# Loading the first eight chunks of a retention kernel in three transfers each, with masks by pairs and a new order of conversions

## The chip, the cores and the metric

The kernel runs on one core of a Trainium2 chip. The metric is the device time of one execution in microseconds (us), the median of several runs. Names of engines: PE is TensorE (matmuls), PEld its weight loads, DVE is VectorE, ACT is ScalarE, POOL is GpSimd, and SP is the engine whose queue issues nearly all loads here.

## What is computed

A retention layer (a linear attention with decay) feeds two dense layers one after the other. Sizes: 4 batches, 8 heads, 768 tokens, head width 64; so 3072 tokens of width 512.

```python
for t in range(S):
    state = gamma[None, :, None, None] * state + np.einsum('bhd,bhe->bhde', k[:, :, t], v[:, :, t])
    y[:, :, t] = scale * np.einsum('bhd,bhde->bhe', q[:, :, t], state)
...
h = x @ w_in                                    # 512 -> 2048
g = np.where(h > 0.0, h, alpha * (np.exp(np.minimum(h, 0.0)) - 1.0))
x = g @ w_out                                   # 2048 -> 512
...
h = np.maximum(np.maximum(x @ w1, x @ w2), x @ w3)   # 512 -> 768, three times
return (h @ w_out).astype(np.float32)
```

The weights arrive as 64-bit floats, and the kernel makes 32-bit ones of them on the chip, as a high and a low part.

## The kernel before

**Chunks.** The retention goes over chunks of 128 tokens with all 8 heads (four pairs); six chunks make a batch, four make a block of 512 tokens for the dense layers. A chunk's tile `x` (1 MB) holds four slots for each pair of heads: queries, keys, keys by token, values by token. For chunk c the kernel forms scores (keys times queries), masks them with the decay table `dmask` (tile `a`), multiplies by the values into `xo` ("mix"; `values` in the later form), adds the state's part by `qd`, the scaled queries ("past"), and carries the state on with an update `up` from `kd`, the scaled keys. `xo` is then split into a high part `xh` (ACT) and a low part `xl` (DVE), which the first dense layer reads.

**Forms.** Chunks 0 to 3 (block 0) use the functions `wide_...`, later ones `open_chunk`, `values`, `finish`, `ready`. The first eight chunks come from an input of their own, `qkv0`, in which the queries lie twice, padded with zeros.

**Weights.** `load_half(n)` loads the n-th half of a weight tile (512 KB) into `raw`, with two buffers. `cv_bits(n)` (ACT) and `cv_rest(n)` (three DVE instructions) turn it into a 32-bit float in `t`, and `cv_rest` then issues the load of half n+2. `cv_high(n)` (ACT) and `cv_low(n)` (DVE) write the two parts into `w`. Halves 0 and 1 serve step f = 0 of the first dense layer, halves 2 and 3 step f = 1, half 4 and on the next ones.

**Dense layer one.** `h1(b, f)` is 12 matmuls of block b with the first half of the weights into `hp`, then on ACT two steps and on DVE one that make `e`, and the split of `e` into `gh` and `gl`. `o1(b, f, ...)` is 12 matmuls with the second half into the accumulators `acc`. On a tile's first use (`fresh`) the passes go in the order in which the parts come ready, the low part of the weights last. `x2_out` copies the four accumulators out at a group's end, and only then can the next group of `o1` begin.

**Order.** The order of the work on every engine up to the last groups is that in which the code is written; every engine runs its own instructions in that order and waits where one isn't ready. The SP queue is in that order too, and each of its transfers waits for the one eight before it to land. PE runs the same list of matmuls throughout: junk products before the first data, chunks 0 to 3, then `h1(0, 0)`, `o1(0, 0)`, `h1(0, 1)`, `o1(0, 1)` with chunks 4 to 7 between them, then `h1(1, 0)`, `h1(1, 1)`, `o1(1, 0)`, `h1(1, 2)` and so on. Past about 200 us nothing of the change is left in the order.

Of the kernel before, what the change touches and what calls it, by code (L numbers as in the profile page):

```python
# [34 lines left out]
def kernel(ctx: ExitStack, tc: tile.TileContext, qkv0, qkv, wa, wb, dmask, qdec, cols, out):  # L35
# [32 lines left out]
    def load(c, part=None):  # L68


        if c >= NCHUNK:
# [4 lines left out]
        if part != 1:
            if c in raw_t:
                return
            if early:
                x = wpool.tile([P, NPAIR, 4, P], F32, tag="w", name="x")  # L80
            else:
                x = ld.tile([P, NPAIR, 4, P], F32, tag="r", name="x")
            raw_t[c] = x
            if early:
                for h, at_, o, n in ((rows(0), 0, 0, 1), (rows(0), 1, 2, 1), (rows(1), 0, 1, 2)):
                    nc.sync.dma_start(
                        out=x[h, :, at_:at_ + n, :].rearrange("d p s t -> d p (s t)"),
                        in_=src[c, :, h, o * P:(o + n) * P].rearrange("p d t -> d p t"),
                    )
            else:  # L90
                for g in range(2):
                    for s in range(2):
                        for p in range(1 if c < 2 * NCH else 2):
                            ps = slice(None) if c < 2 * NCH else slice(p, None, 2)
                            cc = slice((2 * s + (g ^ p)) * P, (2 * s + (g ^ p) + 1) * P)
                            nc.sync.dma_start(
                                out=x[rows(g), ps, s, :], in_=src[c, ps, rows(g), cc].rearrange("p d t -> d p t")
                            )
# [894 lines left out]
```

## Time and profile before

| | before |
|---|---|
| median of 3 runs | 1016.08 us (1013.62 to 1018.23) |
| the profiled execution, its own time | 1016.3 us |
| its span in the trace | 1014.5 us |
| PE busy | 985.0 us, 97% of the span |
| DVE, ACT, POOL busy | 606.2, 348.9, 67.1 us |
| mean granted TensorE clock | 0.996 |

The busy time says who has the most work, not what a change is worth. For that one reads the stretch that the change touches, here the first 80 us or so, and there the idle time of PE and what ended it.

### The profile page before, as it was taken

Reading aid. Unit: us, or ns where it says so; the run is one execution under the profiler, and the core shown is the slowest. Engines: PE = TensorE matmul, PEld = TensorE weight load, DVE = VectorE, ACT = ScalarE, POOL = GpSimd, SP = SyncE. Lnnn points to the kernel's source line nnn. Section 1 sums busy time; section 2 is a strip of 40 time slices with the busy share of each in tenths; the row PEclk is TensorE's granted clock in tenths of the full one; section 3 lists DMA queues with packets and bytes.
Section 4 is the critical chain, followed back from the end, with each engine's and each line's share of the span. In section 5 each row is a group of like instructions: output and inputs, shape, how many; then the busy total and the mean of one; then the engine's idle time right before and its main releaser. Section 6 shows DMA issues by size and latency. Waiting matters only on the chain.

```text
span 1014.5 us, 18210 instructions
## 1 busy us (share of the span) xinstructions
PE 985.0 (97%) x7616; PEld 841.5 (83%) x7616; DVE 606.2 (60%) x1187; ACT 348.9 (34%) x669; POOL 67.1 (7%) x68
## 2 busy tenths in 40 slices
PE   7889999999999999999999999999999999999997
PEld 4667887777888888888888887888999999899996
DVE  2867888744333323333335887997875676757764
ACT  1445555533333333333334665432221121211211
POOL 2410001021111110111100000000000000000000
PEclk9999999999999999999999999999999999999999
DMA  9913364454211211121102444302001020110101
GB/s 236 237 59 103 104 188 161 136 182 127 88 43 43 84 43 42 43 84 43 43 1 87 143 145 146 105 1 83 2 26 58 2 78 6 42 43 1 43 1 42
DMA packets 59010, 79.70 MB, mean 79 GB/s; under 512 B 5168, under 2 KB 40240, under 8 KB 58928
## 3 DMA queue, kind: packets, MB, share of 16 engines
q1 hardware_dynamic: 53168, 68.05, 22.7%
q10 hardware_dynamic: 5760, 10.49, 2.8%
q8 instruction: 60, 0.98, 0.4%
q14 instruction: 22, 0.18, 0.1%
HBM read 63.84 MB, written 14.68 MB: 77 GB/s over the span
## 4 chain that ended last, share of the span: by engine, by line
PE 74%; DVE 13%; DMA 5%; ACT 4%; issue 2%; SPq 1%; POOL 1%; ACTq 0%; DVEq 0%; POOLq 0%
PE hp L612 19%; PE hp L396 19%; PE acc L430 19%; PE acc L661 8%; PE hp L501 5%; DMA raw<-in_wb 3%; DVE t L347 2%; DVE xl L586 1%; ACT gh L408 1%; DVE t L350 1%; DVE e L407 1%; DVE t L619 1%; PE xs L217 1%; PE xs L160 1%; DVE gl L411 1%
## 5 line engine op out<-in xcount | busy, mean ns | idle before, releaser
L396 PE MATMUL hp<-xh,w 128*128 128x512 f32 x768 | 243.7, 390 | 3.8 <-ACT w L361 2.9
L612 PE MATMUL hp<-xh,w 128*128 128x256 f32 x1260 | 232.5, 283 | 2.0 <-DVE e L619 1.6
L430 PE MATMUL acc<-gh,w 128*128 128x512 f32 x768 | 206.4, 397 | 5.6 <-ACT gh L408 3.1
L612 PEld LDWEIGHTS hp<-xh,w 128*128 128x128 f32 x1260 | 198.1, 191 | 4.0 <-issue 1.4
L612 PE MATMUL hp<-xl,w 128*128 128x256 f32 x630 | 178.9, 284 | 1.4 <-DVE xl L586 1.4
L430 PEld LDWEIGHTS acc<-gh,w 128*128 128x128 f32 x768 | 142.7, 189 | 39.8 <-ACT gh L408 4.6
L396 PEld LDWEIGHTS hp<-xh,w 128*128 128x128 f32 x768 | 143.7, 188 | 35.3 <-ACT w L361 4.3
L407 DVE SCALAR_TENSOR_TENSOR e<-e,hp 128x512 f32<-128x512 f32 x96 | 65.8, 685 | 175.9 <-ACT e L404 175.2
L396 PE MATMUL hp<-xl,w 128*128 128x512 f32 x384 | 141.9, 390 | 0.7 <-DVE xl L252 0.7
L612 PEld LDWEIGHTS hp<-xl,w 128*128 128x128 f32 x630 | 120.0, 191 | 4.2 <-DVE xl L586 2.9
L403 ACT ACTIVATE e<-hp 128x512 f32<-128x512 f32 x96 | 57.2, 596 | 171.7 <-PE hp L396 169.2
L430 PE MATMUL acc<-gl,w 128*128 128x512 f32 x384 | 110.9, 390 | 0.3 <-DVE gl L411 0.3
L411 DVE TENSOR_TENSOR gl<-e,gh 128x512 fp32r<-128x512 f32 x96 | 67.3, 701 | 55.9 <-ACT gh L408 54.9
L661 PE MATMUL acc<-w,gh 128*128 128x512 f32 x288 | 90.6, 391 | 0.0
L408 ACT CAST gh<-e 128x512 fp32r<-128x512 f32 x96 | 59.5, 619 | 81.0 <-DVE e L407 79.3
L619 DVE TENSOR_TENSOR t<-hp,m 128x256 f32<-128x256 f32 (+1 forms) x90 | 45.9, 510 | 68.7 <-PE hp L612 68.1
L396 PEld LDWEIGHTS hp<-xl,w 128*128 128x128 f32 x384 | 72.0, 188 | 16.3 <-DVE xl L252 1.0
L430 PEld LDWEIGHTS acc<-gl,w 128*128 128x128 f32 x384 | 72.2, 188 | 16.0 <-DVE gl L411 0.8
L631 ACT COPY m<-hp 128x256 f32<-128x256 f32 x45 | 16.8, 373 | 189.0 <-PE hp L612 115.0
L661 PEld LDWEIGHTS acc<-w,gh 128*128 128x128 f32 x288 | 53.9, 188 | 10.0
L404 ACT ACTIVATE e<-e 128x512 f32<-128x512 f32 x96 | 60.7, 632 | 2.8
L661 PE MATMUL acc<-w,gl 128*128 128x512 f32 x144 | 56.5, 392 | 1.0 <-DVE gl L651 1.0
(100 smaller groups left out, 1048.3 us busy)
## 6 DMA issues: line engine op xcount, KB each, us to landing
raw<-in_wa SPq DMA_DIRECT2D x32, 512.0 KB, 3.7
x<-in_qkv SPq DMA_DIRECT2D x24, 512.0 KB, 5.1
raw<-in_wb SPq DMA_DIRECT2D x24, 512.0 KB, 3.6
x<-in_qkv SPq DMA_DIRECT2D x96, 64.0 KB, 2.4
raw<-x2d SPq DMA_DIRECT2D x12, 512.0 KB, 4.1
out<-o ACTq DMA_DIRECT2D x24, 256.0 KB, 2.1
x<-in_qkv SPq DMA_DIRECT2D x32, 128.0 KB, 4.5
x2d<-o ACTq DMA_DIRECT2D x16, 256.0 KB, 2.2
```

The lines of the kernel that those rows point to most:

```text
L347: nc.vector.scalar_tensor_tensor(out=t, in0=hi, scalar=-0x80000000, in1=t, op0=ALU.bitwise_and, op1=ALU.bitwise_or)
L396: nc.tensor.matmul(hp, w[:, pw, kk * P:(kk + 1) * P], x[px][:, kk, :], start=k == 0, stop=k == len(order) - 1,)
L403: nc.scalar.activation(e, hp, ACTF.Exp)
L404: nc.scalar.activation(e, e, ACTF.Relu, scale=-1.0, bias=1.0)
L407: nc.vector.scalar_tensor_tensor(out=e, in0=e, scalar=-1.0, in1=hp, op0=ALU.mult, op1=ALU.max)
L408: nc.scalar.copy(gh, e)
L411: nc.vector.tensor_tensor(out=gl, in0=e, in1=f32(gh), op=ALU.subtract)
L430: nc.tensor.matmul(acc_t[b][m], w[:, p[0], 512 + m * P:512 + (m + 1) * P], g[p[1]], start=f == f0 and p == first, stop=f == f1 - 1 and p = ...
L501: nc.tensor.matmul(hp, w[:, pw, c0:c0 + P], x[px][:, kk, :], start=k == 0, stop=k == 3 * KDM - 1)
L612: nc.tensor.matmul(o, ws[i][:, pw, kk * P:(kk + 1) * P], xs[i][px][:, kk, :], start=first and k == 0, stop=last and k == 5,)
L619: nc.vector.tensor_tensor(out=out, in0=a, in1=c, op=ALU.add)
L661: nc.tensor.matmul(acc_t[NB + b][m], g[px][:, m * P:(m + 1) * P], w[:, pw, 512:1024], start=f == 0 and i == 0, stop=f == KF2 - 1 and i == 2,)
```

## The change

It has five parts. (1) Each of the first eight chunks is loaded in three transfers and not in four: rows 0 to 63 get queries (128 KB) and then keys, keys by token and values (384 KB); rows 64 to 127 get all four slots in one (512 KB). Before, the first three held queries and keys alone (128, 128 and 256 KB), and the fourth keys by token and values for all 128 rows (512 KB). (2) The scores of a wide chunk lie in four PSUM tiles of two pairs each, and the mask is four DVE instructions of half the size and not two. (3) On PE the update of a wide chunk stands right after the scores, ahead of the mix; junk products after the first scores are 7 and not 8. (4) DVE and ACT get a new order: the low part `xl` of chunk c comes in chunk c+1; conversions of half 1 stand in chunk 3 and those of half 2 ahead of `h1(0, 0)`; the copy of the mask's lower rows stands in chunk 3; in `h1(0, 1)` the mask of chunk 6 and the low part of chunk 5 stand ahead of `cv_low(3)`. (5) At the end of block 0 `finish(7)`, the last of `o1(0, 1)` and `x2_out` stand ahead of the conversion of half 4 and of `h1(1, 0)`.

```diff
+        if early:
+            if c in raw_t:
+                return
+            x = raw_t[c] = wpool.tile([P, NPAIR, 4, P], F32, tag="w", name="x")
+            for h, at_, o in ((rows(0), 0, 0), (rows(0), 1, 2), (rows(1), 0, 1)):
+                n = 1 if o == 0 else 4 - at_
+                nc.sync.dma_start(
+                    out=x[h, :, at_:at_ + n, :].rearrange("d p s t -> d p (s t)"),
+                    in_=qkv0[c, :, h, o * P:(o + n) * P].rearrange("p d t -> d p t"),
+                )
+            return
...
-        sc = sc_t[c] = [ps_acc.tile([P, NPAIR, P], F32, tag="acc", name="sc") for _ in range(2)]
+        sc = sc_t[c] = [[ps_acc.tile([P, 2, P], F32, tag="acc", name="sc") for _ in range(2)] for _ in range(2)]
...
-        for r in range(2):
-            nc.vector.tensor_tensor(
-                out=a[:, r], in0=sc[r], in1=dmask_sb.rearrange("j (p r) i -> j r p i", r=2)[:, r], op=ALU.mult
-            )
+        d = dmask_sb.rearrange("j (p r) i -> j r p i", r=2)
+        for k in range(2):
+            pp = slice(2 * k, 2 * k + 2)
+            for r in range(2):
+                nc.vector.tensor_tensor(out=a[:, r, pp], in0=sc[k][r], in1=d[:, r, pp], op=ALU.mult)
...
     for c in range(CB):
         wide_scores(c)
+        wide_update(c)
+        if c == 0:
+            junk(7)
         wide_mask(c)
-        if c == 0:
-            junk(8)
+        if c:
+            queries_of(c)
+        keys_of(c + 1)
+        wide_state(c)
+        if c:
+            wide_rest(c - 1)
         if c == 2:
             cv_bits(0)
             cv_rest(0)
             load(5)
         if c == 3:
             cv_high(0)
-            wide_rest(2)
             cv_low(0)
-        if c:
-            queries_of(c)
-        if c + 1 < CB:
-            keys_of(c + 1)
+            nc.scalar.copy(dmask_sb[rows(1), :, 0:HC], dmask_sb[rows(1), :, HC:P])
+            cv_bits(1)
+            cv_rest(1)
+            load(6)
+            load(7)
         wide_mix(c)
-        wide_update(c)
-        if c != 2:
-            wide_rest(c)
-    keys_of(4)
-    nc.scalar.copy(dmask_sb[rows(1), :, 0:HC], dmask_sb[rows(1), :, HC:P])
-    cv_bits(1)
+    wide_rest(3)
     later(False)
-    cv_rest(1)
-    load(6)
-    load(7)
-    h1(0, 0, [(ready, 4), (cv_bits, 2)], [(cv_low, 1)], [(open_chunk, 4), (cv_high, 1)])
+    cv_high(1)
+    cv_low(1)
+    cv_bits(2)
+    cv_rest(2)
+    h1(0, 0, [(ready, 4)], [], [(open_chunk, 4)])
     values(4)
-    cv_rest(2)
+    cv_high(2)
+    cv_low(2)
     o1(0, 0, 0, 2)
+    cv_bits(3)
+    cv_rest(3)
     open_chunk(5)
     finish(4)
     ready(5)
-    cv_high(2)
-    cv_low(2)
-    cv_bits(3)
-    cv_rest(3)
-    h1(0, 1, [], [(cv_low, 3), (open_chunk, 6), (finish, 5), (ready, 6)], [(values, 5), (cv_high, 3)])
+    h1(0, 1, [(open_chunk, 6)], [(finish, 5), (cv_low, 3), (ready, 6)], [(values, 5), (cv_high, 3)])
...
     values(7)
+    finish(7)
+    o1(0, 1, 0, 2, (3,))
+    x2_out(0, 0, 2, True)
     cv_bits(4)
     cv_rest(4)
-    o1(0, 1, 0, 2, (3,))
-    finish(7)
     h1(1, 0, [(cv_high, 4)], [(cv_bits, 5)])
-    x2_out(0, 0, 2, True)
     cv_low(4)
     cv_rest(5)
```

Three places show what stands where on the engines. The first is the start of the SP queue, chunks 0 and 1. A row names the transfer's rows, pairs and elements (of 4 bytes); of before:

```order
L86 DMA x<-in_qkv 64x4x128 x2
L86 DMA x<-in_qkv 64x4x256
L694 DMA cols_sb<-in_cols 128x12
L102 DMA x<-in_qkv 128x4x256
L696 DMA dmask_sb<-in_dmask 128x1024
```

and of the change:

```order
L81 DMA x<-in_qkv 64x4x128
L81 DMA x<-in_qkv 64x4x384
L81 DMA x<-in_qkv 64x4x512
L697 DMA cols_sb<-in_cols 128x12
L698 DMA dmask_sb<-in_dmask 128x1024
```

The mask table has one issue fewer in front of it, and the same bytes; no transfer of a chunk now spans all 128 rows.

The second place is DVE from the last steps of chunk 3 to the step that makes `e` of `h1(0, 0)` (L407 before, L410 after); the three rows with `raw` and `t` are one `cv_rest`, `w<-t,w` is `cv_low`. Of before:

```order
L299 TENSOR_TENSOR xl<-xo,xh 128x4x128
L366 TENSOR_TENSOR w<-t,w 128x512
L312 TENSOR_TENSOR state_91<-state_90,cols_sb 128x256
L315 TENSOR_TENSOR state_91<-up,state_91 128x256
L299 TENSOR_TENSOR xl<-xo,xh 128x4x128
L128 RECIPROCAL cols_sb<-cols_sb 128x4
L132 TENSOR_TENSOR qdec_sb<-qdec_sb,cols_sb 128x4x64
L344 TENSOR_SCALAR t<-t 128x512
L347 SCALAR_TENSOR_TENSOR t<-raw,t 128x512
L350 SCALAR_TENSOR_TENSOR t<-raw,t 128x512
L172 TENSOR_TENSOR a<-xs,dmask_sb 128x256 x2
L407 SCALAR_TENSOR_TENSOR e<-e,hp 128x512
```

and of the change, from the conversion of half 1 on:

```order
L347 TENSOR_SCALAR t<-t 128x512
L350 SCALAR_TENSOR_TENSOR t<-raw,t 128x512
L353 SCALAR_TENSOR_TENSOR t<-raw,t 128x512
L300 TENSOR_TENSOR xl<-xo,xh 128x4x128
L126 RECIPROCAL cols_sb<-cols_sb 128x4
L130 TENSOR_TENSOR qdec_sb<-qdec_sb,cols_sb 128x4x64
L369 TENSOR_TENSOR w<-t,w 128x512
L347 TENSOR_SCALAR t<-t 128x512
L350 SCALAR_TENSOR_TENSOR t<-raw,t 128x512
L353 SCALAR_TENSOR_TENSOR t<-raw,t 128x512
L170 TENSOR_TENSOR a<-xs,dmask_sb 128x256 x2
L410 SCALAR_TENSOR_TENSOR e<-e,hp 128x512
```

The conversion of half 1 now stands ahead of the last `xl`, and the low part of half 1 and the conversion of half 2 ahead of `e`; before, those last four stood behind it.

The third place is DVE at the end of block 0: the conversion of half 4, the low part of chunk 7 (L252, L250), `e` and `gl` of `h1(1, 0)`, and the copies of the accumulators (L451, L454). Of before:

```order
L344 TENSOR_SCALAR t<-t 128x512
L347 SCALAR_TENSOR_TENSOR t<-raw,t 128x512
L350 SCALAR_TENSOR_TENSOR t<-raw,t 128x512
L252 TENSOR_TENSOR xl<-xs,xh 128x4x64 x2
L407 SCALAR_TENSOR_TENSOR e<-e,hp 128x512
L411 TENSOR_TENSOR gl<-e,gh 128x512
L451 COPY part<-acc 128x512 x2
```

and of the change:

```order
L250 TENSOR_TENSOR xl<-xs,xh 128x4x64 x2
L454 COPY part<-acc 128x512 x2
L347 TENSOR_SCALAR t<-t 128x512
L350 SCALAR_TENSOR_TENSOR t<-raw,t 128x512
L353 SCALAR_TENSOR_TENSOR t<-raw,t 128x512
L410 SCALAR_TENSOR_TENSOR e<-e,hp 128x512
L414 TENSOR_TENSOR gl<-e,gh 128x512
```

The low part of chunk 7 and the copies moved ahead of the conversion and of the dense step.

## Rows read from the trace of the kernel before

**Rows 1.** The page: busy us of each engine, share of the span, instructions.

```profile
PE 985.0 (97%) x7616; PEld 841.5 (83%) x7616; DVE 606.2 (60%) x1187; ACT 348.9 (34%) x669; POOL 67.1 (7%) x68
```

**Rows 2.** Stretches: length, busy us by engine (instructions), granted clock, DMA share, GB/s.

```profile
10.00:20.00 10.00, 6.50 (x72) 5.54 (x74) 4.01 (x7) 0.59 (x1) 2.48 (x3) 0.83 1.12 262
...
60.00:70.00 10.00, 7.09 (x31) 5.29 (x29) 5.06 (x10) 4.96 (x10) 0.00 (x0) 1.00 0.15 53
```

**Rows 3.** Timeline, PE: start, length, then idle time before and releaser.

```profile
12.39 0.43 PE L282 MATMUL xo<-a,x 128*64 128x128 f32 x2 [2.70 <-DVE a L271]
...
45.08 1.21 PE L396 MATMUL hp<-xh,w 128*128 128x512 f32 x4 [1.28 <-ACT w L361]
...
60.83 0.49 PE L396 MATMUL hp<-xh,w 128*128 128x512 f32 x1 [0.77 <-ACT xh L249]
...
62.04 0.50 PE L396 MATMUL hp<-xl,w 128*128 128x512 f32 x1 [0.71 <-DVE xl L252]
...
69.01 0.70 PE L430 MATMUL acc<-gh,w 128*128 128x512 f32 x2 [1.43 <-DVE part L451]
```

**Rows 4.** Chain of waits: start, length, what.

```profile
7.11 10.10 DMA qdec_sb<-in_qdec
...
17.87 10.25 DMA x<-in_qkv
...
32.35 3.16 PE hp L396 x12
```

**Rows 5.** Timeline: the mask table's arrival, half 0's, an issue, a guard copy.

```profile
3.47 0.43 SPq L102 DMA_DIRECT2D x<-in_qkv  x1
...
11.65 1.29 DVE L271 TENSOR_TENSOR a<-sc,dmask_sb 128x512 f32<-128x512 f32 x2 [10.52 <-DMA dmask_sb<-in_dmask]
...
23.80 0.69 ACT L337 ACTIVATE t<-raw 128x512 f32<-128x512 f32 x1 [2.53 <-DMA raw<-in_wa]
...
58.59 0.26 ACT L240 COPY dmask_sb<-xs 128x1 f32<-128x1 f32 x2 [2.28 <-PE xs L217]
```

**Rows 6.** DMA issues at 11.5 and 17.2 us: size, us to landing.

```profile
x<-in_qkv SPq DMA_DIRECT2D x1, 256.0 KB, 8.1
...
x<-in_qkv SPq DMA_DIRECT2D x1, 256.0 KB, 8.8
```

**Rows 7.** DMA queue, 40 to 45 and 60 to 80 us: packets, MB, share.

```profile
q1 hardware_dynamic: 1591, 1.19, 109.1%
...
q1 hardware_dynamic: 432, 1.57, 23.4%
```

**Rows 8.** Timeline, DVE, 27 to 52 us.

```profile
29.37 1.70 DVE L366 TENSOR_TENSOR w<-t,w 128x512 fp32r<-128x512 f32 x1
...
32.67 0.68 DVE L299 TENSOR_TENSOR xl<-xo,xh 128x512 fp32r<-128x512 f32 x1
...
33.87 0.42 DVE L344 TENSOR_SCALAR t<-t 128x512 int32<-128x512 int32 x1
34.32 0.69 DVE L347 SCALAR_TENSOR_TENSOR t<-raw,t 128x512 int32<-128x512 int32 x1
...
35.05 1.42 DVE L350 SCALAR_TENSOR_TENSOR t<-raw,t 128x512 uint32<-128x512 uint32 x1
...
36.72 0.76 DVE L172 TENSOR_TENSOR a<-xs,dmask_sb 128x256 f32<-128x256 f32 x2 [0.25 <-PE xs L190]
...
37.39 0.68 DVE L407 SCALAR_TENSOR_TENSOR e<-e,hp 128x512 f32<-128x512 f32 x1
...
51.45 0.68 DVE L366 TENSOR_TENSOR w<-t,w 128x512 fp32r<-128x512 f32 x1
```

**Rows 9.** Timeline, POOL.

```profile
29.26 1.27 POOL L149 TENSOR_TENSOR qd<-x,qdec_sb 128x512 f32<-128x512 f32 x1
...
34.33 1.59 POOL L138 TENSOR_TENSOR kd<-x,cols_sb 128x512 f32<-128x512 f32 x1 [3.80 <-DVE t L344]
...
51.97 1.32 POOL L149 TENSOR_TENSOR qd<-x,qdec_sb 128x512 f32<-128x512 f32 x1 [4.80 <-issue]
```

More of the change, by code (lines that the diff above doesn't have):

```diff
@@ L74, in load @@
         early = c < EARLY
-        src = qkv0 if early else qkv
+        if early:
[9 more added lines that the diff above has]
+            return
         if part != 1:
@@ L78, in load @@
                 return
[L79 to L88, printed above, removed]
-                    )
[L90 to L98, printed above, removed]
+            x = raw_t[c] = ld.tile([P, NPAIR, 4, P], F32, tag="r", name="x")
+            for g in range(2):
+                for s in range(2):
+                    for p in range(1 if c < 2 * NCH else 2):
+                        ps = slice(None) if c < 2 * NCH else slice(p, None, 2)
+                        cc = slice((2 * s + (g ^ p)) * P, (2 * s + (g ^ p) + 1) * P)
+                        nc.sync.dma_start(
+                            out=x[rows(g), ps, s, :], in_=qkv[c, ps, rows(g), cc].rearrange("p d t -> d p t")
+                        )
         if part != 0:
             x = raw_t[c]
-            o = 3 * P if early else 4 * P
             nc.sync.dma_start(
                 out=x[:, :, 2:4, :].rearrange("t p s n -> t p (s n)"),
-                in_=src[c, :, :, o:].rearrange("p t n -> t p n"),
+                in_=qkv[c, :, :, 4 * P:].rearrange("p t n -> t p n"),
             )
@@ L262, in wide_scores @@
                 nc.tensor.matmul(
-                    sc[r][:, p, :], x[rows(r), p, 1, :], x[rows(r), p, 0, :], start=p == 0, stop=p == NPAIR - 1
+                    sc[p // 2][r][:, p % 2, :], x[rows(r), p, 1, :], x[rows(r), p, 0, :],
+                    start=p % 2 == 0, stop=p % 2 == 1,
                 )
@@ L269, in wide_mask @@
         sc, a = sc_t.pop(c), wide[0][:, c % 2]
-        for r in range(2):
-            nc.vector.tensor_tensor(
-                out=a[:, r], in0=sc[r], in1=dmask_sb.rearrange("j (p r) i -> j r p i", r=2)[:, r], op=ALU.mult
-            )
+        d = dmask_sb.rearrange("j (p r) i -> j r p i", r=2)
[3 more added lines that the diff above has]
+                nc.vector.tensor_tensor(out=a[:, r, pp], in0=sc[k][r], in1=d[:, r, pp], op=ALU.mult)
         a_t[c] = a
@@ L278, in wide_mix @@
         a = a_t.pop(c)
+        qd = st_t.pop(c)[0]
         xo = xo_t[c] = ps_h.tile([P, NPAIR, P], F32, tag="h", name="xo")
@@ L286, in wide_mix @@
         if c:
-            qd = st_t[c][0]
             for p in range(NPAIR):
@@ L294, in wide_mix @@
         nc.scalar.copy(x_t[0][0][:, :, c * P:(c + 1) * P], xo)
+        del raw_t[c]
     def wide_rest(c):
@@ L301, in wide_update @@
     def wide_update(c):
-        kd = st_t.pop(c)[1]
-        v = raw_t.pop(c)[:, :, 3, :].rearrange("t p (r d) -> t p r d", r=2)
-        up = ps_h.tile([P, NPAIR, D], F32, tag="h", name="up")
+        kd = st_t[c][1]
+        v = raw_t[c][:, :, 3, :].rearrange("t p (r d) -> t p r d", r=2)
+        up = up_t[c] = ps_h.tile([P, NPAIR, D], F32, tag="h", name="up")
         for p in range(NPAIR):
@@ L307, in wide_update, with wide_state @@
                 nc.tensor.matmul(up[rows(r), p, :], kd[:, p, r, :], v[:, p, r, :], start=p == 0, stop=p == NPAIR - 1)
-        new, old = state[c % 2], state[1 - c % 2]
+    def wide_state(c):
+        new, old, up = state[c % 2], state[1 - c % 2], up_t.pop(c)
         if c == 0:
@@ L692 @@
     start.__enter__()
-    load(0, 0)
+    load(0)
     nc.sync.dma_start(out=cols_sb[:, 0:H + NPAIR], in_=cols)
-    load(0, 1)
     nc.sync.dma_start(out=dmask_sb, in_=dmask)
```

## Prediction

> **What bounds the kernel now.** The page first: PE is busy for 985.0 us, 97% of the span [rows 1], so over the whole run only idle time of PE is to be won, some 30 us, and the change touches no later order than that of the first 80 us. The table by stretch shows the two kinds of idle time there. From 10 to 20 us PE is busy for 6.50 of 10 us while the DMA share stands at 1.12, which is as full as it gets; from 60 to 70 us PE is busy for 7.09 of 10 with a DMA share of 0.15 [rows 2]. So the start waits for data, and the later stretch for engines. The chain of waits says the same: a transfer of chunk 3 (17.87 + 10.25 = 28.1 us) and then the short way to the first dense product at 32.35 [rows 4]. PE's own rows give the places and prices of the later waits: 1.28 us at 45.08 for the high weights of half 2, 0.77 and 0.71 us at 60.83 and 62.04 for the split of chunk 7, 1.43 us at 69.01 for the copies of the accumulators [rows 3]. These four, 4.2 us, and whatever comes off the 32 us of the start are what the change can win.
>
> **Step 1, the loads.** Bytes stay as they are. One issue goes per chunk, 0.43 us on SP ahead of the mask table [rows 5]. The table lands at 11.6 now [rows 5]. Half of the issue gap of chunk 0 should go too, since its larger pieces are issued earlier; I take 10.6 us (estimate, bounds 11.2, only the issue saved, and 10.2).
>
> From there to the last of chunk 3 the queue is full: 28.1 - 11.6 = 16.5 us for three chunks, a table and a weight half. One chunk costs 4.3 us: half 0 is there at 23.8 [rows 5], chunk 3 at 28.1. What the new shapes cost no row shows, so bounds. Below: time of a packet by its size. From 40 to 45 us a packet (748 B in the mean) took 109.1% x 16 x 5 / 1591 = 55 ns, from 60 to 80 us (3634 B) 23.4% x 16 x 20 / 432 = 173 ns [rows 7]; the line through both gives 45, 66, 87 and 108 ns for 512, 1024, 1536 and 2048 B. A chunk is 512 packets of 512 B and 768 of 1 KB now, 74 us, and would be 256 each of 512, 1536 and 2048 B, 62 us: 17% less, 3.6 us a chunk. Above: the pieces of 64 rows. In chunk 3 the three of them (512 KB) end at 17.2 + 8.8 = 26.0 us, 2.2 us after half 0, and the 128-row piece of the same 512 KB takes the other 2.1; in chunk 2 they end at 11.5 + 8.1 = 19.6, 2.4 us after the table that landed at 7.11 + 10.10 = 17.2 [rows 4 to 6]. All pieces span 64 rows after the change, so twice 2.2 to 2.4, that is 4.4 to 4.8 us. I take 4.3, no change: the larger packets and the lost 128-row piece pull against each other, and both rows lie within 0.1 to 0.5 of it. Chunk 3 then lands at 10.6 + 16.5 = 27.1 us, 1.0 earlier; bounds 27.1 - 4 x 0.7 = 24.3 (chunks 0 to 3 at 3.6) and 27.1 + 4 x 0.5 = 29.1 (at 4.8).
>
> [...]
>
> Scores now wait for the whole chunk, where they waited for three of its four pieces. Behind them on PE stand update and mix, and for these DVE. That, and masks by pairs, the update ahead of the mix, and junk of 7, cost or win nothing up to chunk 3: while chunk c+1 is still coming, PE is done with chunk c (it waits 2.70 us at 12.39 already [rows 3]). If the loads no longer covered it, the four smaller masks would cost 0.2 us a chunk.
>
> **Step 2, DVE from chunk 3 to e.** Today `e` of h1(0, 0) ends at 37.39 + 0.68 = 38.1 us [rows 8], and o1(0, 0) follows it. In the new order DVE has, from the first half of chunk 3's scores (0.6 us after landing, estimate): four masks as two pairs of 0.76, two state steps of 0.4, `xl` 0.7, `cv_low` 0.7, a conversion 0.42 + 0.69 + 0.69 = 1.8, `xl` with the two small steps up to 33.87 in 1.2, `cv_low` 0.7, a conversion 1.8, the mask of chunk 4 0.76, `e` 0.68: 10.7 us in one row [rows 8]. Beside it run `kd` and `qd` of chunk 4 on POOL, and these collide: the third step of a conversion took 1.42 and not 0.69 us beside a `kd` that itself took 1.59, and `cv_low` 1.70 and not 0.68 beside a `qd` of 1.27 [rows 8, 9]. Two such collisions, 0.7 to 1.0 each, 1.5 in all. Together 12.8 us (11.3 without, 13.5 with more). ACT (copy of the mask's rows, a conversion, `xh`) and PE are done before DVE comes to their products. So `e` ends at 27.1 + 12.8 = 39.9: **+1.8 us**. The loads' win is spent here: half 1's low part and half 2's conversion, 2.5 us, now stand ahead of `e`. The loads that conversions issue move with them: that of half 3 goes out earlier than now, and chunks 6 and 7 behind it on SP, all of them ahead of need.
>
> [...]
>
> **Step 3, h1(0, 1).** It waits 1.28 us for the high weights of half 2 [rows 3]. These are converted before `e` now and cast while o1(0, 0) runs: **-1.2 us**. The same work is thus paid in step 2 and won here.
>
> **Step 4, cv_low(3).** It runs at 51.45 in 0.68 us, ahead of the `qd` that POOL starts at 51.97 [rows 8, 9]. Behind mask 6 and `xl` of chunk 5 it starts after that `qd` and is blocked until its end, some 0.5 + 1.3 us later, and the last two products of that piece of o1(0, 1) wait for it: **+0.6 us** (0 to 1.2).
>
> **Step 5, the end of block 0.** The waits of 0.77, 0.71 and 1.43 us [rows 3] go: three products of o1(0, 1) cover the split of chunk 7, and the copies come two h1 earlier. Given back: the guard copy of 0.26 us [rows 5], which those products covered, and some 0.4 us where halves 5 and 6, converted later against PE now, are just late; the load of half 6, which the conversion of half 4 issues, moves back with it. **-2.2 us** (-2.9 to -1.5).
>
> Past 80 us PE has weights waiting as before, so what is won stays.
>
> **Sum.** +1.8 - 1.2 + 0.6 - 2.2 = -1.0 us against the profiled execution's own 1016.3 us, which lies 0.2 above the median of the runs shown: 1015.3.
>
> **Rivals.**
> - *Larger packets set the rate.* For it: the line through [rows 7]. Against it: pieces of 512 B and 1 KB differ little in the rows of landing. Chunk 3 lands at 24.3, `e` ends 1.0 us earlier than now, sum -3.8: 1012.5. Without any collision on POOL and with all of step 5 it would reach some 1010.
> - *Half-width transfers set the rate, and it ends slower than before.* Place: every chunk's third piece. For it: chunk 2's 2.4 us. At 4.8 a chunk, chunk 3 lands at 29.1, `e` ends 3.8 us later than now, sum +1.0: 1017.3. It decides from about 4.55 us a chunk; for over 0.5% slower it would take 5.8. [...]
> - *DVE and POOL collide more often.* For it: DVE has no pause left ahead of `e`. Two more collisions there and a full one at step 4, +2.2 on the forecast: 1017.5.
> - *The orders are hidden, nothing changes.* If `e` came no later and step 5's waits only moved on to halves 5 and 6: 1016.
>
> **Numbers.** A measurement of this kernel can tell about 0.5% (5 us) from no change. Forecast 0.50, its own range 1013.8 to 1016.8; larger packets 0.22; half-width 0.15; collisions 0.08; nothing 0.05. The runs shown spread by 2 us around their median, which the range takes in: 1011.0 to 1018.2, with about 0.1 left out on either side. Under 1011.2 I see only the first rival with more luck, 0.12; over 1021.2 only the second at a far lower rate, 0.03; within 0.5% the rest, 0.85.
>
> **What would show it.** Step 1: the start of `kd` of chunk 3 near 27.1 (24.3 or 29.1 for the rivals). Step 2: L410 ending near 40, with no idle time on DVE ahead of it. Step 3: no wait of PE for ACT's weights ahead of h1(0, 1). Step 4: a `cv_low` of over 1.2 us beside a `qd` near 52. Step 5: the first product of o1(1, 0) some 5.7 us after the first of h1(1, 0) (8.2 now), with no wait for the copies. The forecast is wrong if a chunk lands in under 4.0 or over 4.6 us, or if DVE idles ahead of `e`.

## The result and the profile after

The change makes the kernel slower: 1024.67 us median (1024.10 to 1026.17) against 1015.11 us of the kernel before (four runs of each), a ratio of 1.0086 (95% interval 1.0063 to 1.0109). The prediction was 1015.3 us, range 1011.0 to 1018.2; it was wrong. The profiled execution took 1024.49 us with a span of 1022.4 us, 7.9 more than before.

The page after, busy time and granted clock in 40 slices (answers to [rows 1]):

```profile
PE 990.4 (97%) x7615; PEld 845.0 (83%) x7615; DVE 605.2 (59%) x1195; ACT 348.8 (34%) x669; POOL 66.9 (7%) x68
...
PEclk8799999999999999999999999999999999999999
```

PE is busy for 5.4 us more with one junk product fewer: part of the loss is not waiting but slower running, in the first two slices (51 us), whose digits of the granted clock are 8 and 7 (every digit was 9 before). The stretches (columns as in [rows 2]):

```profile
10.00:20.00 10.00, 10.00 (x113) 6.85 (x110) 4.62 (x12) 0.58 (x1) 2.68 (x3) 0.74 1.11 220
40.00:50.00 10.00, 7.40 (x70) 5.82 (x73) 7.54 (x13) 2.91 (x7) 1.04 (x1) 0.66 1.10 221
```

From 10 to 20 us the queue is as full as before (share 1.11) but moves 220 GB/s, not 262 [rows 2]; from 40 to 50 us the granted clock is 0.66, where it was 1.00. PE's timeline shows where the time goes (answers to [rows 3]):

```profile
28.95 2.04 PE L260 MATMUL sc<-x 64*128 64x128 f32 x14 [2.32 <-DMA x<-in_qkv]
...
41.99 0.32 PE L228 MATMUL xs<-a,x 64*64 64x64 f32 x2 [2.63 <-DVE a L170]
...
44.83 2.07 PE L433 MATMUL acc<-gh,w 128*128 128x512 f32 x4
...
51.91 0.27 PE L215 MATMUL xs<-qd,dmask_sb 64*64 64x64 f32 x1 [0.53 <-issue]
...
52.17 1.19 PE L399 MATMUL hp<-xh,w 128*128 128x512 f32 x4
...
62.02 0.73 PE L433 MATMUL acc<-gh,w 128*128 128x512 f32 x2 [0.95 <-DVE w L369]
...
69.52 0.50 PE L399 MATMUL hp<-xh,w 128*128 128x512 f32 x1
```

PE waits 2.32 us for chunk 3, then 2.63 us ahead of the values of chunk 4; behind that, four products of o1(0, 0) take 2.07 us, where four of the same shape take 1.19 in h1(0, 1). The old wait ahead of h1(0, 1) (1.28 us [rows 3]) is gone, and so are the three at the end of block 0. What PE waited for at 41.99 is on DVE and ACT:

```profile
38.99 0.67 ACT L340 ACTIVATE t<-raw 128x512 f32<-128x512 f32 x1 [2.83 <-DMA raw<-in_wa]
```

```profile
39.69 0.46 DVE L347 TENSOR_SCALAR t<-t 128x512 int32<-128x512 int32 x1 [1.52 <-ACT t L340]
...
42.19 0.68 DVE L410 SCALAR_TENSOR_TENSOR e<-e,hp 128x512 f32<-128x512 f32 x1
...
60.86 1.11 DVE L369 TENSOR_TENSOR w<-t,w 128x512 fp32r<-128x512 f32 x1
```

The first row is `cv_bits(2)`: ACT stands for 2.83 us until half 2 has landed, DVE then idles 1.52 us, and `e`, behind that conversion and a mask, ends at 42.87 (38.07 before [rows 8]). The last row is `cv_low(3)`, 1.11 us where it took 0.68 [rows 8], and PE's wait at 62.02 is for it. On POOL the starts of `kd` of chunks 1, 2 and 3 tell when each chunk is complete:

```profile
15.71 1.04 POOL L136 TENSOR_TENSOR kd<-x,cols_sb 128x512 f32<-128x512 f32 x1 [5.30 <-DMA x<-in_qkv]
...
21.48 1.04 POOL L136 TENSOR_TENSOR kd<-x,cols_sb 128x512 f32<-128x512 f32 x1 [3.50 <-DMA x<-in_qkv]
...
28.95 1.04 POOL L136 TENSOR_TENSOR kd<-x,cols_sb 128x512 f32<-128x512 f32 x1 [5.19 <-DMA x<-in_qkv]
```

Between them the mask table is there at 10.60 and half 0 at 22.82 (answers to [rows 5]):

```profile
10.60 1.42 DVE L273 TENSOR_TENSOR a<-sc,dmask_sb 128x256 f32<-128x256 f32 x4 [9.47 <-DMA dmask_sb<-in_dmask]
```

```profile
22.82 0.70 ACT L340 ACTIVATE t<-raw 128x512 f32<-128x512 f32 x1 [2.07 <-DMA raw<-in_wa]
```

How far the changed kernel is behind the old one, place by place:

| place | before | after | behind by |
|---|---|---|---|
| `e` of h1(0, 0) ends | 38.07 | 42.87 | 4.8 |
| o1(0, 0) ends | 42.2 | 49.9 | 7.7 |
| h1(0, 1) starts | 45.08 | 52.17 | 7.1 |
| first piece of o1(0, 1) starts | 51.76 | 59.62 | 7.9 |
| first piece of o1(0, 1) ends | 53.43 | 62.75 | 9.3 |
| h1(1, 3) starts | 78.0 | 84.8 | 6.8 |
| end of span | 1014.5 | 1022.4 | 7.9 |

### The profile page after: what moved, and what is told of

Same layout as the page of the kernel before. It is cut to its first block, busy times and chain, and to the rows that moved or that the text cites. A ratio compares the mean times of both kernels' runs of the same rounds, so it can differ in the third digit from the quotient of the medians.

```text
span 1022.4 us, 18201 instructions
## 1 busy us (share of the span) xinstructions
PE 990.4 (97%) x7615; PEld 845.0 (83%) x7615; DVE 605.2 (59%) x1195; ACT 348.8 (34%) x669; POOL 66.9 (7%) x68
## 4 chain that ended last, share of the span: by engine, by line
PE 73%; DVE 13%; DMA 7%; ACT 4%; issue 2%; POOL 1%; ACTq 0%; SPq 0%; DVEq 0%; POOLq 0%
PE hp L615 19%; PE acc L433 19%; PE hp L399 18%; PE acc L664 8%; PE hp L504 5%; DMA raw<-in_wb 3%; DMA x<-in_qkv 2%; DVE t L350 2%; DVE xl L589 1%; ACT gh L411 1%; DVE e L410 1%; DVE t L353 1%; PE xs L215 1%; DMA raw<-in_wa 1%; DVE t L622 1%
## 5 line engine op out<-in xcount | busy, mean ns | idle before, releaser
L410 DVE SCALAR_TENSOR_TENSOR e<-e,hp 128x512 f32<-128x512 f32 x96 | 65.8, 686 | 176.6 <-ACT e L407 173.7
L433 PEld LDWEIGHTS acc<-gl,w 128*128 128x128 f32 x384 | 73.1, 191 | 16.5 <-DVE gl L414 1.1
L622 DVE TENSOR_TENSOR t<-hp,m 128x256 f32<-128x256 f32 (+1 forms) x90 | 45.9, 510 | 68.9 <-PE hp L615 68.2
L407 ACT ACTIVATE e<-e 128x512 f32<-128x512 f32 x96 | 60.7, 632 | 2.8
```

Source lines behind the costliest of these rows:

```text
L407: nc.scalar.activation(e, e, ACTF.Relu, scale=-1.0, bias=1.0)
L410: nc.vector.scalar_tensor_tensor(out=e, in0=e, scalar=-1.0, in1=hp, op0=ALU.mult, op1=ALU.max)
L433: nc.tensor.matmul(acc_t[b][m], w[:, p[0], 512 + m * P:512 + (m + 1) * P], g[p[1]], start=f == f0 and p == first, stop=f == f1 - 1 and p = ...
L622: nc.vector.tensor_tensor(out=out, in0=a, in1=c, op=ALU.add)
```

## The experiments

Two theories stood at the start. **A:** pieces on 64 rows load at a lower rate, and the new order makes `e` wait for half 2, which that makes late. **B:** the new order is too long by itself. "Ratio" is to the kernel before, estimated from all runs, with its 95% interval; it differs by up to 0.2% from the quotient of the medians, so differences of 1 or 2 us between two experiments are not firm.

**E1, old transfers in the changed kernel.**

```diff
-            for h, at_, o in ((rows(0), 0, 0), (rows(0), 1, 2), (rows(1), 0, 1)):
+            for h, at_, o, n in ((rows(0), 0, 0, 1), (rows(0), 1, 2, 1), (rows(1), 0, 1, 2)):
...
+                    out=raw_t[c][:, :, 2:4, :].rearrange("t p s n -> t p (s n)"),
+                    in_=qkv0[c, :, :, 3 * P:].rearrange("p t n -> t p n"),
```

> The changed kernel with the four old transfers of each early chunk and everything else of the change. Theory A (half-width transfers bring half 2 late, and the new order makes e wait for it): chunk 3 lands near 27.5 us, half 2 near 36, DVE does not idle ahead of e, which ends near 40 (42.9 in the changed kernel); TensorE is granted 1.00 from 42 to 50 us (0.50 in the changed kernel); time 1014 to 1017. Rival B (the new order alone is too long): e ends at 42 or later, time 1022 or more. Rival C (masks by pairs and the update ahead of the mix cost it): late already at chunk 3, time 1020 or more.

Measured 1021.42, ratio 1.0060 (1.0038 to 1.0083): A's number is missed, and B and C are left (E10 is on C). `e` ended at 41.7, with DVE still waiting for half 2:

```profile
38.45 0.56 DVE L352 TENSOR_SCALAR t<-t 128x512 int32<-128x512 int32 x1 [2.43 <-ACT t L345]
```

So the new order costs about 6 us without the new loads, and A's cause (the wait for half 2) is in it, even at the old loads: half 2 landed at 37.7 in this execution.

**E2, new transfers in the kernel before** (the `load` of the change, the rest as it was).

> The kernel before with the three new transfers of each early chunk and nothing else. Theory A: half 2 lands 3 us later as in the changed kernel, but in the old order its conversion stands behind e, so only chunk 3 (+0.8), half 1 (+1.5) and chunk 4 (+2.0) count: e ends 1.5 to 2.5 us later, no idle stretch of TensorE of over 2 us, time 1016.5 to 1019. If the transfers alone cost it (rival D): 1023 or more. If the order alone costs it (rival B): no change, 1015.

Measured 1025.35, ratio 1.0111 (1.0086 to 1.0135): A's size was far too small, B's "no change" is out, and D fits. The new loads alone cost more than the whole change. In the trace 3.7 us are lost at the start of h1(0, 1) (48.81) and 8.6 at that of h1(1, 0) (69.4; 60.8 before): between them PE stood for 2.04 us for "issue" (the last section) and then ran at a granted clock of 0.50 from 56.6 to 63.3 us.

**E3, transfers of 128 rows in the changed kernel.** The same three per chunk; the input holds the queries once.

```diff
-            for h, at_, o in ((rows(0), 0, 0), (rows(0), 1, 2), (rows(1), 0, 1)):
+            for p, at_, n in ((slice(0, 4), 0, 1), (slice(0, 2), 1, 3), (slice(2, 4), 1, 3)):
...
-                    out=x[h, :, at_:at_ + n, :].rearrange("d p s t -> d p (s t)"),
+                    out=x[:, p, at_:at_ + n, :].rearrange("d p s t -> d p (s t)"),
```

> The changed kernel, again three transfers for each early chunk and the same bytes, but each transfer spans all 128 rows (512 packets of 512 B and 512 of 1536 B a chunk, where the changed kernel has 256 each of 512, 1536 and 2048 B); the input is laid out for that without the padding zeros. Theory A with the rows as the cause: a chunk takes 4.1 to 4.4 us, chunk 3 lands at 26.5 to 27.5, half 2 near 35.5, e ends near 40, time 1013 to 1016. If the number of transfers or the size of the packets is the cause (rival E): chunk 3 near 29, half 2 near 39, time 1023 to 1025.

Measured 1016.04, ratio 1.0005 (0.9984 to 1.0026), 8 to 9 us less than the changed kernel, as A had it with the rows as the cause (the new input is a rival; see E12). Its stretch, and PE in h1(0, 0):

```profile
10.00:20.00 10.00, 9.74 (x154) 8.06 (x152) 6.85 (x18) 2.45 (x4) 4.55 (x4) 1.00 1.08 364
```

```profile
24.79 1.19 PE L398 MATMUL hp<-xh,w 128*128 128x512 f32 x4 [0.69 <-ACT xh L293]
28.30 1.20 PE L398 MATMUL hp<-xl,w 128*128 128x512 f32 x4 [2.32 <-DVE xl L299]
```

364 GB/s against 220, with smaller packets. h1(0, 0) starts 10 us earlier than in the changed kernel, yet the total is that of the kernel before: with the loads out of the way the new order shows its own waits, the first of 2.32 us for the low part of chunk 3.

**E4, the conversion of half 2 behind `e`,** new loads.

```diff
-    cv_bits(2)
-    cv_rest(2)
-    h1(0, 0, [(ready, 4)], [], [(open_chunk, 4)])
+    h1(0, 0, [(ready, 4), (cv_bits, 2)], [], [(open_chunk, 4)])
     values(4)
-    cv_high(2)
-    cv_low(2)
+    cv_rest(2)
     o1(0, 0, 0, 2)
+    cv_high(2)
+    cv_low(2)
```

> The changed kernel with the conversion of half 2 behind e, as it stood before; the loads are the new ones. Theory A: e no longer waits for half 2 and ends near 40 (42.9 in the changed kernel), TensorE waits under 1.5 us ahead of it and is granted 1.00 in o1(0, 0); time 1016 to 1019. Rival B' (the other parts of the new order cost it): e still at 42 or later, 1022 or more. Rival F (the clock alone, whatever e does): the grant still falls to 0.50 near 42 us, time 1021 or more.

Measured 1023.64, ratio 1.0100 (1.0071 to 1.0129): a miss. `e` ended at 41.1 and o1(0, 0) ran at the full clock (granted 1.00), as A had it, but PE then waited 3.23 us at 49.93 for nothing that the profile shows ("issue"; the last section). What was saved was lost again at the next place.

**E5, the end of block 0 alone** (part 5 in the kernel before).

> The kernel before with the last part of the change alone: the end of chunk 7, the last piece of o1(0, 1) and the copies of the accumulators stand ahead of the conversion of half 4 and of h1(1, 0). If step 5 holds on its own, the waits of 0.77, 0.71 and 1.43 us go and the time falls by 1.5 to 2.9: 1012.3 to 1013.7. Rival (the waits move to halves 5 and 6): no change, 1015. It also gives a second trace of the old loads in the old order: half 2 near 36.0 and chunk 5 near 39 if what the first trace shows is typical; near 37.7 and 42 (as in the run with the old loads in the new order) if executions differ by that much.

Measured 1013.60, ratio 0.9976 (0.9953 to 1.0000): 2.4 us less, as step 5 had it. Its trace holds a warning:

```profile
10.00:20.00 10.00, 6.12 (x70) 5.14 (x72) 4.89 (x7) 0.59 (x1) 3.00 (x3) 0.83 1.14 228
```

```profile
51.15 1.20 PE L396 MATMUL hp<-xh,w 128*128 128x512 f32 x4 [1.28 <-ACT w L361]
```

Up to here it is the kernel before, transfer for transfer, and this execution moved 228 GB/s and not 262 [rows 2], and reached h1(0, 1) at 51.15 and not 45.08 [rows 3]; it took 1017.68 us, 4 over its own median. The rate of the same loads differs that much between executions, so sizes are taken from medians here, and only large differences from single traces.

**E6, TensorE kept busy.** Junk products in two waits of the changed kernel.

```diff
+        if c == 3:
+            junk(8, ps_acc, "acc")
         wide_scores(c)
...
+    junk(10, ps_acc, "acc")
     values(4)
```

> The changed kernel with junk matmuls added in two of TensorE's waits: 8 ahead of the scores of chunk 3 and 10 ahead of the values of chunk 4 (about 2 us each), into accumulators that are free there. If the fall of the granted clock is what costs the time (theory clock): 1.00 granted from 42 to 50 us, o1(0, 0) takes 3.0 and not 5.1 us, and the time falls by 2 to 3: 1021.5 to 1022.5. If what comes later sets the time anyway (chunk 5, half 3, and TensorE's own code, whose block arrived at 49 us in the changed kernel with TensorE going on at 51.9): the clock stays up, but h1(0, 1) still starts at 51.5 or later and the time is 1024 to 1025.

Measured 1023.08, ratio 1.0069 (1.0043 to 1.0095): between the two and not told apart from the changed kernel. The stretches, then PE, then the DMA queues at 55.0 to 55.2 us (packets, MB, share):

```profile
40.00:50.00 10.00, 8.88 (x153) 6.68 (x151) 7.51 (x16) 2.70 (x7) 2.91 (x3) 1.00 1.09 225
50.00:60.00 10.00, 5.47 (x135) 4.59 (x134) 1.98 (x4) 2.75 (x8) 1.23 (x2) 0.77 0.62 145
```

```profile
48.29 1.17 PE L399 MATMUL hp<-xh,w 128*128 128x512 f32 x4 [0.52 <-ACT xh L247]
...
57.93 0.79 PE L188 MATMUL xs<-x,kd 64*64 64x64 f32 x17 [3.65 <-issue]
```

```profile
q8 instruction: 1, 0.02, 47.3%
```

The clock was granted in full (1.00 from 40 to 50 us), o1(0, 0) took 3.0 us, and h1(0, 1) started 3.9 us earlier than in the changed kernel (48.29 and 52.17); 1.2 of these were there at the end of `e` already (41.69 and 42.87). Then PE stood for 3.65 us, the clock fell (0.77 from 50 to 60 us), and o1(0, 1) began at 59.6 in both. In these two traces the clock's part is thus at most 2.7 us at that place, and it is given back at the next.

**E7, 128-row transfers and part 5 in the order of before** (E3's load, E5's end).

> The kernel before in its own order, with 128-row transfers for the early chunks (three each) and the last part of the change. Theory A (half-width loads are the bound of the first 50 us, the new order only adds to DVE ahead of e): chunk 3 near 20 us, e of h1(0, 0) near 30 to 32 (38.1 before, 34.3 in the new order with 128-row transfers), h1(0, 1) near 38 to 40, and with the last part another 2 us: 1006 to 1010, faster than both kernels. Rival (the new order is better once the loads are fast): 1014 or more.

Measured 1011.05, ratio 0.9948 (0.9928 to 0.9968): faster than both kernels, though 1 us short of A: `e` ended at 34.2, not 30 to 32. The old order within the chunks is now a limit:

```profile
18.78 0.43 PE L279 MATMUL xo<-a,x 128*64 128x128 f32 x2 [0.78 <-DVE a L268]
...
24.43 0.43 PE L279 MATMUL xo<-a,x 128*64 128x128 f32 x2 [1.23 <-DVE a L268]
```

PE waits for each chunk's mask, and a chunk takes 5.1 to 5.8 us though its data is there (the scores of chunk 3 start at 22.0, its last transfer landed near 20).

**E8, E3 with half 2 late** (E3's load and E4's order).

> The changed kernel with 128-row transfers and the conversion of half 2 behind e. Theory A: with the loads early, DVE's own chain sets e; three conversion steps less ahead of it (3.0 us, 3.6 beside GpSimd) bring e from 34.3 to about 31 and h1(0, 1) from 41.6 to 38.5 to 40.5; time 1012 to 1015. If e is not what sets the time there: no change from 1016.

Measured 1014.78, ratio 0.9977 (0.9957 to 0.9997): within the expectation, 1.3 us less than E3 by the medians and 2.8 by the ratios, whose intervals overlap. `e` ended at 32.9 and not 31.

**E9, a mixture.** 128-row transfers, the new order within chunks 0 to 3, the old order of the conversions and of h1(0, 1), part 5. Against E3 it differs in this only:

```diff
-            cv_bits(1)
-            cv_rest(1)
-            load(6)
-            load(7)
         wide_mix(c)
     wide_rest(3)
+    cv_bits(1)
     later(False)
-    cv_high(1)
-    cv_low(1)
-    cv_bits(2)
-    cv_rest(2)
-    h1(0, 0, [(ready, 4)], [], [(open_chunk, 4)])
+    cv_rest(1)
+    load(6)
+    load(7)
+    h1(0, 0, [(ready, 4), (cv_bits, 2)], [(cv_low, 1)], [(open_chunk, 4), (cv_high, 1)])
...
-    h1(0, 1, [(open_chunk, 6)], [(finish, 5), (cv_low, 3), (ready, 6)], [(values, 5), (cv_high, 3)])
+    h1(0, 1, [], [(cv_low, 3), (open_chunk, 6), (finish, 5), (ready, 6)], [(values, 5), (cv_high, 3)])
```

(and `cv_rest(2)`, `cv_high(2)`, `cv_low(2)`, `cv_bits(3)`, `cv_rest(3)` where they stood before).

> 128-row transfers, the new order within chunks 0 to 3 (masks by pairs, update ahead of the mix, low part one chunk later), the order of before from there to the end of block 0 (conversion of half 1 behind the low part of chunk 3, half 2 behind e), and the new end of block 0. With the loads early, the old chunks take 5.2 us each on TensorE and the new ones 4.0, and the old order of the conversions keeps the 2.3 us wait for the low part of chunk 3 away. Theory A (loads first, then DVE's and TensorE's own chains): h1(0, 0) near 25, e near 30 to 31 (34.2 in the run with 128-row transfers in the old order), h1(0, 1) near 39; 1007 to 1010. Rival (the wait only moves on to the weights of half 2 and to TensorE's code): no gain over that run, 1011.

Measured 1007.76, ratio 0.9924 (0.9907 to 0.9940): the fastest kernel. The order of the conversions and of h1(0, 1), which is part 4 without what it changes within the chunks, thus costs 8 us (0.9924 to 1.0005). With fast loads the new order within the chunks wins 2.4 by the ratios (0.9948 to 0.9924), with intervals that overlap. In h1(0, 0) no wait stands between the passes any more:

```profile
25.49 1.20 PE L398 MATMUL hp<-xh,w 128*128 128x512 f32 x4 [0.69 <-ACT xh L293]
26.52 1.08 PE L398 MATMUL hp<-xl,w 128*128 128x512 f32 x4
```

**E10, the new order within chunks 0 to 3 alone,** old transfers, everything else as before.

> The kernel before, old transfers, with only the new order within chunks 0 to 3. Theory: the update ahead of the mix makes TensorE wait for kd of chunk 3, which needs the fourth transfer of the chunk, and the mix stands behind it: h1(0, 0) 1 to 2 us later, no more; 1016 to 1019. If this is where the new order cost 6 us with the old loads: 1020 or more. As step 1 of the prediction had it, nothing: 1015 to 1016.

Measured 1016.83, ratio 1.0008 (0.9989 to 1.0026). PE does wait for `kd` (1.65 us at 28.39), but h1(0, 0) starts at 31.66: nothing is lost that these runs could tell, as step 1 had it, and E1's rival C falls.

**E11, E1 with half 2 late** (old transfers, E4's order).

> The changed kernel with the old transfers and the conversion of half 2 behind e. Theory A (with the old loads the new order costs 6 us mainly since e waits for half 2, 2.4 us on DVE, and the granted clock falls after it): 2 to 5 less than the 1021.4 of the changed kernel with the old transfers, 1016.5 to 1019.5, and no fall of the clock in o1(0, 0). Rival (the conversions of half 1 or the chunks cost it): 1020 or more.

Measured 1019.71, ratio 1.0030 (1.0010 to 1.0050): 1.7 less than E1 by the medians, just outside A's range, and 3.0 by the ratios. Half 2 is a part of the 6 us; how large a part is not known better than that.

**E12, even and odd rows.** E3's input; three transfers of 64 rows with the packets of the changed kernel.

```diff
-            for h, at_, o in ((rows(0), 0, 0), (rows(0), 1, 2), (rows(1), 0, 1)):
+            for h, at_, n in ((slice(0, P, 2), 0, 1), (slice(0, P, 2), 1, 3), (slice(1, P, 2), 0, 4)):
```

> The changed kernel with the same three transfers for each early chunk (64 rows each, 256 packets each of 512, 1536 and 2048 B), but the first two take the even rows and the third the odd rows of all 128, where the changed kernel has rows 0 to 63 and rows 64 to 127. If it is the place of the rows that halves the rate: as with 128-row transfers, some 360 GB/s from 10 to 20 us, chunk 3 near 20 us, 1014 to 1017. If 64 rows in a transfer are too few wherever they lie: 220 to 230 GB/s, chunk 3 near 29, 1023 to 1025.

Measured 1015.69, ratio 0.9999 (0.9985 to 1.0012). Its stretch, and `kd` of chunks 1 to 3:

```profile
10.00:20.00 10.00, 9.51 (x148) 7.82 (x147) 6.30 (x17) 1.87 (x3) 4.57 (x4) 1.00 1.06 386
```

```profile
12.51 1.04 POOL L135 TENSOR_TENSOR kd<-x,cols_sb 128x512 f32<-128x512 f32 x1 [3.82 <-DMA x<-in_qkv]
...
16.08 1.04 POOL L135 TENSOR_TENSOR kd<-x,cols_sb 128x512 f32<-128x512 f32 x1 [1.28 <-DMA x<-in_qkv]
...
21.09 1.52 POOL L135 TENSOR_TENSOR kd<-x,cols_sb 128x512 f32<-128x512 f32 x1 [2.73 <-DMA x<-in_qkv]
```

386 GB/s with the same shapes: neither the 64 rows as a number nor the packets cost the rate. That leaves the place of the rows, 0 to 63 or 64 to 127, or the input, which is new in E3, E7 to E9 and E12 to E15 alike. No run loads half-rows from the new input, but the trace of the kernel before speaks against the input:

```profile
43.00:43.50 0.50, 0.50 (x36) 0.50 (x30) 0.11 (x1) 0.00 (x0) 0.00 (x0) 1.00 1.07 347
44.00:45.00 1.00, 0.00 (x0) 0.00 (x0) 0.87 (x4) 1.00 (x4) 1.00 (x2) 1.00 1.23 180
```

Both stretches move chunks of the old input alone, with a full queue. In the first it is mostly the piece of chunk 6 on all 128 rows (196 packets, 0.17 MB; it landed at 45.4), at 347 GB/s; in the second mostly the queries of chunk 7 on rows 0 to 63 (330 packets, 0.18 MB; they landed at 45.8 and 46.4), at 180. So the old input is not slow where all rows are written, and the place of the rows is left. Why it decides is not shown.

**E13 to E15, the pieces of part 4,** each added alone to E9.

E13, the order in h1(0, 1):

```diff
-    h1(0, 1, [], [(cv_low, 3), (open_chunk, 6), (finish, 5), (ready, 6)], [(values, 5), (cv_high, 3)])
+    h1(0, 1, [(open_chunk, 6)], [(finish, 5), (cv_low, 3), (ready, 6)], [(values, 5), (cv_high, 3)])
```

> The fastest kernel so far (128-row transfers, new order within the chunks, old order of the conversions, new end of block 0; 1007.8) with the new order in h1(0, 1) added: the mask of chunk 6 and the low part of chunk 5 ahead of the low part of half 3. As step 4 of the prediction had it: +0.6, 1008.4. By the waits in the traces with that order (1.35 us for gl and 0.72 us for the low part, first piece of o1(0, 1) 4.3 and not 1.6 us): +2.5 to 3.5, 1010.3 to 1011.3.

E14, half 2 ahead of `e`:

```diff
+    cv_bits(2)
+    cv_rest(2)
-    h1(0, 0, [(ready, 4), (cv_bits, 2)], [(cv_low, 1)], [(open_chunk, 4), (cv_high, 1)])
+    h1(0, 0, [(ready, 4)], [(cv_low, 1)], [(open_chunk, 4), (cv_high, 1)])
     values(4)
-    cv_rest(2)
+    cv_high(2)
+    cv_low(2)
...
-    cv_high(2)
-    cv_low(2)
```

> The same kernel (1007.8) with the conversion of half 2 ahead of e of h1(0, 0) added. As steps 2 and 3 of the prediction had it: e later by the conversion's 1.8 us, and h1(0, 1) earlier by the 1.2 us for which it waits for half 2's high weights, so +0.6. By the run that took it back (1016.0 to 1014.8): +1.3, 1009. If beside GpSimd's kd and qd the three steps take 3.6 us: e 3 us later, +2 to 3.

E15, half 1 in chunk 3 and ahead of h1(0, 0):

```diff
+            cv_bits(1)
+            cv_rest(1)
+            load(6)
+            load(7)
         wide_mix(c)
     wide_rest(3)
-    cv_bits(1)
     later(False)
-    cv_rest(1)
-    load(6)
-    load(7)
-    h1(0, 0, [(ready, 4), (cv_bits, 2)], [(cv_low, 1)], [(open_chunk, 4), (cv_high, 1)])
+    cv_high(1)
+    cv_low(1)
+    h1(0, 0, [(ready, 4), (cv_bits, 2)], [], [(open_chunk, 4)])
```

> The same kernel (1007.8) with the conversion of half 1 in chunk 3, ahead of the low part of chunk 3, and its low part ahead of h1(0, 0). By the traces: TensorE waits 2.3 us for the low part of chunk 3 in the middle of h1(0, 0), but the conversion no longer stands ahead of e, so e is late by only 0.5 to 1.5 us: +1 to 2, 1009 to 1010. If the three pieces have to make up the 8 us between them: +3 to 4, 1011 to 1012.

Measured 1012.52, 1012.11 and 1012.20; ratios 0.9950 (0.9929 to 0.9971), 0.9947 (0.9927 to 0.9968) and 0.9935 (0.9914 to 0.9957). Against E9's 0.9924 that is 2.6, 2.3 and 1.1 us, 6 of the 8 together; the medians lie 4.8, 4.4 and 4.4 us above E9's. Each piece costs something, but with intervals of some 2 us to either side the shares, and whether they add up to the 8, are not known. E13 on DVE, POOL and PE:

```profile
45.48 1.71 DVE L413 TENSOR_TENSOR gl<-e,gh 128x512 fp32r<-128x512 f32 x1
```

```profile
45.37 1.27 POOL L146 TENSOR_TENSOR qd<-x,qdec_sb 128x512 f32<-128x512 f32 x1 [4.83 <-issue]
```

```profile
47.25 0.73 PE L432 MATMUL acc<-gl,w 128*128 128x512 f32 x2 [1.35 <-DVE gl L413]
48.69 0.73 PE L432 MATMUL acc<-gh,w 128*128 128x512 f32 x2 [0.71 <-DVE w L368]
```

With the mask of chunk 6 ahead of it, `gl` meets the `qd` of POOL and takes 1.71 us (0.69 in E9), and PE waits for it and then for the low part. In E14 PE waits for the chain with half 2 in it, and then runs at half clock (0.53 from 35 to 40 us):

```profile
32.52 0.32 PE L227 MATMUL xs<-a,x 64*64 64x64 f32 x2 [3.13 <-DVE a L169]
35.36 2.07 PE L432 MATMUL acc<-gh,w 128*128 128x512 f32 x4
```

```profile
35.00:40.00 5.00, 5.00 (x19) 3.89 (x16) 1.08 (x2) 0.84 (x3) 0.00 (x0) 0.53 1.01 341
```

**Together,** ratios to the kernel before:

| early chunks | order of before | new order (parts 2 to 5) |
|---|---|---|
| four transfers, as before | 1 | 1.0060 (E1) |
| three of rows 0-63 or 64-127 | 1.0111 (E2) | 1.0086 (the change) |
| three of 128 rows | 0.9948 (E7, with part 5) | 1.0005 (E3) |

The costs don't add up. As the traces read, with the slow loads both orders wait for data, and a wait that is paid there is not paid again for DVE; the new order then comes out no worse (2.5 us ahead, about what part 5 wins, with intervals that overlap). With 128-row loads its parts 2 to 4 cost 5.8.

## Why the prediction was wrong

**Step 1, the price of a chunk, is the step that failed.** It took 4.3 us, between 3.6 and 4.8, since rows of either sign lay within 0.5. The mask table came at 10.6, as forecast; from there to chunk 3 at 28.95 it took 18.3 us and not 16.5. That is 0.6 more for each of the three chunks, some 4.9 us, and by the two rows from which the 4.3 was read (half 0 at 22.82, chunk 3 at 28.95) 6.1. So chunk 3 came where the rival "half-width transfers" had it (29.1), and that rival's mechanism decided (E3, E12). The reading failed in its method: the time from one landing to the next is not the price of the later piece, since transfers overlap (before, half 0 was issued at 12.9, and the last piece of chunk 2 landed only at 21.6). Half 0, the same transfer in both kernels, landed 2.2 us behind chunk 2 before and 1.5 behind it after (21.6 and 23.8, 21.3 and 22.8 by the DMA issues). A stretch in which mostly one sort of piece moves told more: the 180 GB/s of half-row pieces from 44 to 45 us (shown under E12) would have made 5.8 us of a chunk, too much, but far past the 4.55 from which that rival decides; the changed kernel's 220 GB/s make 4.8. The 4.3 also came from one execution, and the same loads in another were slower (E5).

The second error is a term at nothing: no step asked when half 2 lands; ACT was taken to be done before DVE comes to its products, and the loads behind half 2 to be "all of them ahead of need". In step 2's own sum DVE comes to half 2's conversion at 36.7 (39.9 less conversion, mask and `e`), and ACT must have the half 0.7 earlier, at 36.0, which is when it landed before; there was no slack. At the lower rate it landed 2.9 us later (38.9 by the DMA issues), and ACT waited 2.83 us for it; half 3 landed 5.2 later (45.9 and 40.7). The rival's 1017.3 was too low as well: the loads alone cost 11 us (E2).

**Step 2** had `e` end at 39.9; it ended 3.0 later: 1.85 for chunk 3, and 1.52 for which DVE idled ahead of `e`, the sign that the prediction itself named as its refutation. DVE's own sum was fair otherwise. What was left out is the granted clock: after its wait of 2.63 us PE was granted 0.50 from 42.5 to 49 us, and o1(0, 0) took 5.07 and not 3.03 us. This wait of PE cost more than its length, and no term of the sum held that.

**Step 3** was right in its mechanism: the wait for half 2's high weights went. PE gained 0.6 and not 1.2 there, since 0.53 us of "issue" came in its place.

**Step 4** had the right place and too small a size: 0.6 predicted, 1.5 in the trace after (7.9 behind at the start of the piece, 9.3 at its end), and 2.6 by the ratio alone (E13), where `gl` was held up beside `qd` and PE waited for `cv_low(3)` behind it. That an instruction of DVE is held until the one on POOL ends, from which the 0.6 was worked out, was the author's estimate, and no run shows it as a rule: in the trace after, `cv_low(3)` began beside a `qd` and ended 0.55 us behind it (61.97 and 61.42), but `xl` took 0.75 us beside the same `qd` and 0.76 at 69.22 with POOL at rest.

**Step 5** was right: -2.2 predicted, -2.5 in the trace (9.3 to 6.8 behind), -2.4 alone (E5).

The sum by these steps in the profile: +4.80 to `e`, +2.86 for the clock and the way to the end of o1(0, 0), -0.57 (step 3), +0.77 ahead of o1(0, 1), where PE stood for 0.62 us at 59.00 with no releaser, +1.46 (step 4), -2.54 (step 5): +6.78 at 85 us. The last 1.1 us of the span lie later and are left open. That the change's loss hangs on the rows of its loads is shown by E2, E3 and E12; how E2's 11 us divide between late data, waits with no releaser and the clock is read from one trace and not shown apart.

## What to carry to other kernels

Here a transfer's price hung on which rows it writes (217 to 220 GB/s for halves, 362 to 386 for rows of both halves): keep every large load on all 128 rows or on rows spread over both halves. Price a shape from a stretch in which it moves nearly alone, not from the gap between two landings, and by an experiment of its own where the rows of the profile bracket the point at which it decides. Work moved ahead of a critical step takes that step's place behind every load it needs itself, so ask when its data lands at the worst rate in the range. Where a wait goes, look at the next one (a wait with no releaser, the clock, the following load) before the gain is booked: several of the savings here were lost within 10 us.

## What the runs showed of the hardware

**Waits of PE with no releaser.** In twelve traces (the changed kernel, E1 to E4, E6, E8, E9, E11 to E13, E15) PE stood for 0.5 to 3.7 us with no releaser, and each time one packet on the queue "q8 instruction" had moved 2.3 to 3.0 us ahead of the end of that wait: at 55.1 in E6 with PE going on at 57.93, at 54.4 in E2 with this row:

```profile
57.09 0.37 PE L188 MATMUL xs<-x,kd 64*64 64x64 f32 x1 [2.04 <-issue]
```

Other packets of that queue had no such wait behind them: in the kernel before one at 37.2, when the DMA share was 0.35, but also one at 48.4, when it was 1.18. That the packet is a load of PE's own code, as two of the expectations have it, and that full data queues make it late, is the author's guess from the times and not shown; no run moved it on purpose.

**The rate of the same loads** differed between executions: 228 to 264 GB/s from 10 to 20 us in traces with the old transfers (262 [rows 2], E1 234, E5 228, E10 264, E11 261); with rows 0 to 63 and 64 to 127 apart it was 217 to 220 (the changed kernel, E2, E4, E6), and with rows spread over both halves 362 to 386 (E3, E7 to E9, E12 to E15).
